# Attention and two MLPs on one core: a new order for the first batch, with its values and the second batch's keys summed by TensorE

## The chip, the cores and the metric

One core of one Trainium2 chip runs the whole program in one launch. The metric is the device time in microseconds; the kernel before was timed three times, with a median of 1646.4 us (1645.67 to 1647.27).

## The reference

```python
k_p = k.reshape(B, H, Sp, 8, D).mean(axis=3)      # B 8, H 8, S 576, D 64, Sp 72
v_p = v.reshape(B, H, Sp, 8, D).mean(axis=3)
scores = scale * np.matmul(q, k_p.transpose(0, 1, 3, 2))
attn = softmax(scores)
x = np.matmul(attn, v_p)                          # to [4608, 512]
x = np.maximum(0.01 * h, h) @ w_out               # h = x @ w_in, 512 -> 2048 -> 512
out = (r * r) @ w_out2                            # r = max(x @ w_in2, 0)
```

All is in float32. Keys and values are averaged over groups of eight rows before the attention.

## The kernel before, in words

The program has three stages: attention (eight batches), the first MLP and the second MLP. Their work is interleaved: the first MLP walks over tiles of 512 tokens and 16 slices of the weights (`first`, L316 to L318 into `h`, and `second`, L316 to L318 into `acc`), and between its slices the loop draws steps from the generator `attention()` at a fixed rate. The first batch has nothing to hide behind, since the first MLP needs its result. Its order is written out by hand in `first_batch`, and `in_order` binds the instructions of every engine to that written order.

For one batch, 576 queries go in five chunks that start at 0, 128, 256, 320 and 448; the tile names carry this number. The keys of a batch come as two main tiles of 128 rows by 2 by 512 (`k`, L408) and a rest of four small loads (`rk`, L403), since 72 pooled rows for each of two heads are 16 more than 128. `pooled` adds eight rows to one with three VectorE additions (L368, L374). `pooled_pe` does the same on TensorE: for each main tile it adds eight products with the identity matrix in PSUM (`kp` and `vp`, L381), which the trace records as 16 matmuls. `prepare_k` then transposes the sums (`trk`, `trr`, L422, L437) and copies them into `kT`.

Stage a transposes a chunk of queries (`trq`, L540), and ScalarE copies it to `qT` (L544). The steps of `stage_parts`, called `b(i)` in the list, are: scores on TensorE (`s`, L561); the maximum on VectorE (`mx`, L571); eight exponentials on ScalarE (L578); sum, reciprocal (L590, L591) and the products `p` on GpSimd (L593, L601). `c1` and `c2` transpose `p` back (`pt`, `pr`) and split it into a high part by ScalarE and a low part by VectorE (L614, L615, L626, L628). `d` multiplies with the values (`o`), and L652 and L657 split the result into `xh` and `xl`, which `first` reads. `w(f)` is one step of decoding weight slice f: L204, L208, L211, L215 and L225 on VectorE and L224 on ScalarE. `split_weights` makes the two parts of a slice (`hl_in`, L243, L244).

Loads are issued by SyncE's queue, except the first main keys, which ScalarE's queue issues. `first_batch` uses VectorE for the first keys and values; the second batch's keys and values are summed on TensorE (`K_ON_PE`, `V_ON_PE`), at that time between the matmuls of the first MLP.

Of the kernel before, what the change touches and what calls it, by code (L numbers as in the profile page):

```python
# [17 lines left out]
P = 128  # L18
# [14 lines left out]
def attention_two_mlps(  # L33
# [21 lines left out]
    NF = DFF // P  # L55
    SPANS = (320, 256)
    EARLY = 5
    V_ON_PE = (1,)
    K_ON_PE = (1,)
    AHEAD = 5  # L60
    RATES = (2.5, 5.25)
# [259 lines left out]
    def attention():  # L321

        with ExitStack() as s:
# [70 lines left out]
            def load_kv(b, src, nm, issue=None):  # L394

                groups = src[b].rearrange("(m a) (kk j) d -> (a kk) m (j d)", a=2, j=POOL)
                rest = kv_tile(b, NP * RX, 1, f"r{nm}{b}")
                main = [kv_tile(b, P, 2, f"{nm}{b}_{g}") for g in range(2)]
                KV[nm, b] = rest, main

                def load_rest():
                    for m in range(NP):
                        nc.sync.dma_start(out=rest[m * RX:(m + 1) * RX, 0], in_=groups[P:, m])  # L403

                if nm == "v" or b == 0:
                    load_rest()
                for g in range(2):
                    (issue or nc.sync).dma_start(out=main[g], in_=groups[0:P, 2 * g:2 * g + 2])  # L408
                if nm == "k" and b > 0:
                    load_rest()  # L410

            KV = {}

# [7 lines left out]
            def turned(tr, kd, m):  # L421
                nc.tensor.transpose(tr[:, m * P:(m + 1) * P], kd[:, m].rearrange("p i d -> p (i d)"), ident)  # L422
# [20 lines left out]
            def prepare_k(b):  # L443
                kr, kk = KV.pop(("k", b))
                i = b % 2
                kd = ap1.tile([P, NP, 2, D], F32, tag="kd", name=f"kd{b}")
                if b == 0:
                    pooled(rr[:, 1:2], kr)
                if b in K_ON_PE:
                    for ps in pooled_pe(f"kp{b}", kk):  # L450
                        yield
                    nc.scalar.copy(kd, ps.unsqueeze(2).to_broadcast([P, NP, 2, D]))
                else:
                    for g in range(2):
                        pooled(kd[:, 2 * g:2 * g + 2], kk[g])
                        if b > 0:
                            yield
                            continue
                        tr = work("trk0") if g == 0 else tr
                        for m in range(2 * g, 2 * g + 2):  # L460
                            turned(tr, kd, m)
                        yield
                if b > 0:
                    pooled(rr[:, 1:2], kr)
                    load_v(b)
                    tr = work(f"trk{b}")
                    for m in range(NP):
                        turned(tr, kd, m)
                put_keys(i, tr, slice(0, NP))
                put_rest(i, b)  # L470
                yield
# [57 lines left out]

            qn, qt = {}, {}  # L530

            def load_q(b, span, at, off, n):
                qn[b, at] = qp.tile([P, H, D], F32, tag="q", name=f"q{b}_{at}", bufs=3)
                nc.sync.dma_start(out=qn[b, at][:n], in_=q[b, :, at:at + n, :].rearrange("h p d -> p h d"))

            def stage_a(b, span, at, off, n):
                t = qn.pop((b, at))
# [130 lines left out]

            nch = len(chunks) // B

            def first_batch():
# [4 lines left out]
                def q_in(i):  # L676
                    load_q(*chunks[i])
# [12 lines left out]
                def c2(i):  # L690
                    rest_part(*chunks[i])

                def d(i):
                    if i not in rows:
                        rows[i] = stage_d(*chunks[i][:2])
                    next(rows[i])
                    put_stores(made)

                def w(f):
                    if f not in dec:  # L700
                        dec[f] = decode_steps(f)
                    next(dec[f], None)

                def fetch(f):
                    RAW[f] = fetch_weights(1, [("in", f), ("out", f)])

                load_k(0)
                q_in(0)
                q_in(1)
                load_v(0)  # L710
                q_in(2)
                next(pk)
                a(0)
                next(pk)
                next(pk)
                a(1)
                q_in(3)
                q_in(4)
                fetch(0)
                next(pv)  # L720
                fetch(1)
                b(0)
                b(0)
                b(1)
                b(1)
                b(0)
                next(pv)
                b(1)
                b(0)
                a(2)  # L730
                next(pv)
                b(1)
                a(3)
                b(2)
                b(2)
                next(pv)
                b(2)
                b(2)
                c1(0)
                b(3)  # L740
                b(3)
                c2(0)
                c1(1)
                c2(1)
                next(pv)
                a(4)
                q_in(5)
                q_in(6)
                q_in(7)
                load_k(1)  # L750
                c1(2)
                c2(2)
                b(3)
                b(4)
                b(4)
                w(0)
                b(3)
                d(0)
                d(0)
                b(4)  # L760
                w(0)
                b(4)
                d(0)
                d(0)
                w(0)
                w(0)
                fetch(2)
                c1(3)
                c2(3)
                c1(4)  # L770
                c2(4)
                split_weights("in", 0, 0)
                w(1)
                w(1)
# [12 lines left out]
                w(2)  # L787
                w(2)
                a(5)
                a(6)  # L790
# [1 line left out]
            marks.append(in_order(first_batch))  # L792
            ready[0] = 1
            yield
            yield from prepare_k(1)
            stage_b(*chunks[nch])
            yield
            def finish(i):
# [516 lines left out]
```

## Time and profile before

| | |
|---|---|
| median of 3 runs | 1646.4 us |
| the profiled execution | 1644.78 us |
| its span | 1643.1 us |
| TensorE busy in the span | 1604.8 us (98%) |
| VectorE busy | 1391.3 us (85%) |
| ScalarE busy | 1006.9 us (61%) |
| first matmul of the first MLP | at 43.85 us |

The span is what the instructions fill; 1.7 us of the execution lie around it. Busy time of TensorE holds time in which a matmul waits in its pipeline, so what matters is where it stands idle. In the first 44 us it is often idle, and from then on hardly ever.

### The profile page before, as it was taken

The page shows a single profiled execution, that of the slowest core. Times are in us where ns is not written, and L with a number is a line of the kernel's source. Part 1 is how long each engine was busy: PE and PEld are TensorE (multiplying, and loading weights), DVE is VectorE, ACT ScalarE, POOL GpSimd, SP SyncE. Part 2 cuts the span into 40 slices and gives each one's busy share as a digit, 9 for nine tenths or more (in the row PEclk, how much of TensorE's full clock was granted, in tenths as well). Part 3 has the DMA queues.
Part 4 walks back from the last instruction along what each step waited for, and adds up shares of the span by engine and source line. Part 5 has one row for each costly group of instructions (what it writes and reads, how often), then busy time and mean ns, then how long its engine had stood idle before and what let it go on. Part 6 is the DMA issues. An engine that isn't in the chain of part 4 may idle for free.

```text
span 1643.1 us, 25946 instructions
## 1 busy us (share of the span) xinstructions
PE 1604.8 (98%) x9048; PEld 1469.3 (89%) x9048; DVE 1391.3 (85%) x2062; ACT 1006.9 (61%) x1922; POOL 122.8 (7%) x152
## 2 busy tenths in 40 slices
PE   5999999999999999999999999999999999999999
PEld 4877788888888999999999998998998998998997
DVE  6999776889889989979759589789789799799687
ACT  6787677755667867667556546446456456455454
POOL 4121232213210000000000000000000000000000
PEclk9999999999999999999999999999999999999999
DMA  7665445776647689887766755865865766756655
GB/s 210 201 200 156 145 137 155 219 221 208 187 147 266 244 273 303 256 308 226 226 195 202 235 185 143 287 193 148 274 189 173 259 180 193 243 173 207 198 167 167
DMA packets 223090, 340.94 MB, mean 207 GB/s; under 512 B 55536, under 2 KB 137456, under 8 KB 222960
## 3 DMA queue, kind: packets, MB, share of 16 engines
q1 hardware_dynamic: 222416, 338.23, 66.3%
q8 instruction: 72, 1.18, 0.3%
q10 hardware_dynamic: 544, 1.05, 0.2%
q14 instruction: 58, 0.48, 0.1%
HBM read 268.44 MB, written 69.21 MB: 205 GB/s over the span
## 4 chain that ended last, share of the span: by engine, by line
PE 79%; DVE 11%; ACT 4%; DMA 3%; issue 2%; SPq 0%; POOL 0%; DVEq 0%; ACTq 0%; POOLq 0%
PE psum L1087 14%; PE psum L316 13%; PE psum L318 13%; PE psum L317 13%; PE psum L1088 7%; PE h L316 3%; PE h L318 2%; PE h L317 2%; PE acc L317 2%; PE acc L318 2%; PE acc L316 2%; ACT x L578 2%; DMA wb_in<-ws_in 1%; PE s L561 1%; DVE gl L874 1%
## 5 line engine op out<-in xcount | busy, mean ns | idle before, releaser
L1087 PE MATMUL psum<-wb_out,oh 128*128 128x512 f32 x1008 | 352.9, 394 | 0.0
L316 PE MATMUL psum<-xh,wb_in 128*128 128x384 f32 x1008 | 337.4, 335 | 3.1 <-ACT s L1061 1.5
L318 PE MATMUL psum<-xh,wb_in 128*128 128x384 f32 x1008 | 336.8, 334 | 0.0
L317 PE MATMUL psum<-xl,wb_in 128*128 128x384 f32 x1008 | 336.8, 334 | 0.0
L939 ACT CAST oh<-g 128x768 fp32r<-128x768 f32 x252 | 210.1, 836 | 157.5 <-PE psum L1087 91.1
L1088 PE MATMUL psum<-wb_out,ol 128*128 128x256 f32 x1008 | 281.8, 280 | 0.0
L940 DVE TENSOR_TENSOR ol<-g,oh 128x768 fp32r<-128x768 f32 x252 | 238.7, 951 | 16.3 <-ACT oh L939 14.1
L1087 PEld LDWEIGHTS psum<-wb_out,oh 128*128 128x128 f32 x1008 | 189.6, 188 | 43.3
L316 PEld LDWEIGHTS psum<-xh,wb_in 128*128 128x128 f32 x1008 | 189.2, 188 | 5.0 <-DVE g L1067 2.0
L317 PEld LDWEIGHTS psum<-xl,wb_in 128*128 128x128 f32 x1008 | 189.2, 188 | 0.2
L318 PEld LDWEIGHTS psum<-xh,wb_in 128*128 128x128 f32 x1008 | 189.2, 188 | 0.0
L1088 PEld LDWEIGHTS psum<-wb_out,ol 128*128 128x128 f32 x1008 | 188.8, 187 | 0.2
L993 ACT CAST wb_in<-wb_in 128x512 fp32r<-128x512 f32 x144 | 89.3, 621 | 146.3 <-DMA wb_in<-ws_in 142.2
L994 DVE TENSOR_TENSOR wb_in<-wb_in 128x512 fp32r<-128x512 f32 x144 | 98.5, 687 | 81.4 <-ACT wb_in L993 81.2
L943 DVE TENSOR_TENSOR g<-g,g 128x768 f32<-128x768 f32 x144 | 135.7, 950 | 1.5 <-ACT g L1015 0.9
L316 PE MATMUL h<-xh,hl_in 128*128 128x512 f32 (+1 forms) x320 | 121.5, 380 | 2.7 <-ACT hl_in L243 1.0
L317 PE MATMUL acc<-gl,hl_out 128*128 128x512 f32 (+1 forms) x320 | 119.0, 374 | 3.0 <-DVE gl L874 3.0
L316 PE MATMUL acc<-gh,hl_out 128*128 128x512 f32 (+1 forms) x320 | 121.0, 384 | 0.8 <-ACT gh L873 0.7
L318 PE MATMUL acc<-gh,hl_out 128*128 128x512 f32 (+1 forms) x320 | 118.7, 374 | 0.0
L318 PE MATMUL h<-xh,hl_in 128*128 128x512 f32 (+1 forms) x320 | 118.7, 371 | 0.0
L317 PE MATMUL h<-xl,hl_in 128*128 128x512 f32 (+1 forms) x320 | 118.0, 369 | 0.0
L317 PE MATMUL psum<-ol,wb_out 128*128 128x384 f32 x336 | 112.6, 335 | 0.0
(162 smaller groups left out, 3122.8 us busy)
## 6 DMA issues: line engine op xcount, KB each, us to landing
wb_in<-wd_in SPq DMA_DIRECT2D x108, 512.0 KB, 3.7
wb_out<-wd_out SPq DMA_DIRECT2D x108, 512.0 KB, 4.4
wb_in<-ws_in SPq DMA_DIRECT2D x144, 256.0 KB, 3.1
wb_out<-ws_out SPq DMA_DIRECT2D x144, 256.0 KB, 2.7
xs<-x SPq DMA_DIRECT2D x18, 768.0 KB, 5.6
out_dram<-o SPq DMA_DIRECT2D x23, 384.0 KB, 5.3
q<-in_q_dram SPq DMA_DIRECT2D x32, 256.0 KB, 3.8
v<-in_v_dram SPq DMA_DIRECT2D x16, 512.0 KB, 4.2
```

The source lines that it names most:

```text
L316: nc.tensor.matmul(outp, ah, bh, start=first, stop=False, **kw)
L317: nc.tensor.matmul(outp, ah, bl, start=False, stop=False, **kw)
L318: nc.tensor.matmul(outp, al, bh, start=False, stop=last, **kw)
L561: nc.tensor.matmul(sc[:n, 2 * m:2 * m + 2].rearrange("p a x -> p (a x)"), qT[:, 2 * e + m, :n], kT[b % 2][:, 2 * e + m].rearrange("p a x - ...
L578: nc.scalar.activation(x[:n, 4 * e + h], sc[:n, h], AF.Exp, bias=mx[:n, h], accum_out=sm[:n, 4 * e + h],)
L939: nc.scalar.copy(hi, src)
L940: nc.vector.tensor_tensor(out=lo, in0=src, in1=raw(hi), op=ALU.subtract)
L943: nc.vector.tensor_tensor(out=out_, in0=a, in1=b, op=ALU.subtract)
L993: nc.scalar.copy(whole[:, 0], raw(whole[:, 1]))
L994: nc.vector.tensor_tensor(out=whole[:, 1], in0=raw(whole[:, 1]), in1=raw(whole[:, 0]), op=ALU.subtract)
L1087: nc.tensor.matmul(outp, ah, b, start=first, stop=False, skip_group_check=True)
L1088: nc.tensor.matmul(outp[:, 1], al, b[:, 0], start=False, stop=last, skip_group_check=True)
```

## The change

The loads of the main keys and values go ahead of their rests, and the first chunk of queries is issued by ScalarE's queue. VectorE sums the main keys first and the rest after them. TensorE begins with 18 transposes of the identity matrix into a tile that nobody reads (`run_in`). The values of the first batch are summed on TensorE (`vp`), and so are the keys of the second batch (`kp`) before the first MLP begins. The written order of the first batch is new.

```diff
-    V_ON_PE = (1,)
+    V_ON_PE = (0, 1)
...
-                if nm == "v" or b == 0:
-                    load_rest()
                 for g in range(2):
                     (issue or nc.sync).dma_start(out=main[g], in_=groups[0:P, 2 * g:2 * g + 2])
-                if nm == "k" and b > 0:
-                    load_rest()
+                for m in range(NP):
+                    nc.sync.dma_start(out=rest[m * RX:(m + 1) * RX, 0], in_=groups[P:, m])
...
-                if b == 0:
-                    pooled(rr[:, 1:2], kr)
...
-                        tr = work("trk0") if g == 0 else tr
-                        for m in range(2 * g, 2 * g + 2):
-                            turned(tr, kd, m)
-                        yield
-                if b > 0:
-                    pooled(rr[:, 1:2], kr)
+                pooled(rr[:, 1:2], kr)
+                if b == 0:
+                    yield
+                else:
                     load_v(b)
...
+                def run_in(n):
+                    idle = work("run_in")[:, 0:P]
+                    for _ in range(n):
+                        nc.tensor.transpose(idle, ident, ident)
...
                 load_k(0)
-                q_in(0)
+                q_in(0, nc.scalar)
                 q_in(1)
                 load_v(0)
+                run_in(18)
...
+                load_k(1)
+                pk1.append(prepare_k(1))
...
-            yield from prepare_k(1)
+            yield from pk1[0]
```

The line numbers fall by 11 in the part that the prediction speaks of (L561 becomes L550). Three places show the new order. First TensorE, between the scores of the second chunk and the transposes of the third. Before:

```order
L561 MATMUL s_128_0_294<-kT_184,qT_128_252 128x144 x2
L561 MATMUL s_128_1_297<-kT_184,qT_128_252 128x144 x2
L540 MATMUL trq_256_329<-ident,q_256_218 128x64 x4
L540 MATMUL trq_320_345<-ident,q_320_254 128x128 x4
L561 MATMUL s_256_0_355<-kT_184,qT_256_334 64x144 x2
```

And now:

```order
L550 MATMUL s_128_0_296<-kT_184,qT_128_271 128x144 x2
L550 MATMUL s_128_1_299<-kT_184,qT_128_271 128x144 x2
L381 MATMUL vp_330<-v_0_210,ident 128x128 x8
L381 MATMUL vp_330<-v_1_211,ident 128x128 x8
L529 MATMUL trq_256_347<-ident,q_256_237 128x64 x4
L550 MATMUL s_256_0_371<-kT_184,qT_256_352 64x144 x2
```

The sums of the values stand ahead of the third chunk's transposes. Next ScalarE, from the exponentials of the first chunk to those of the third. Before:

```order
L578 ACTIVATE x_0_278,sm_0_279<-s_0_1_284,mx_0_1_289 128x72 x4
L578 ACTIVATE x_128_291,sm_128_292<-s_128_0_294,mx_128_0_300 128x72 x4
L578 ACTIVATE x_128_291,sm_128_292<-s_128_1_297,mx_128_1_302 128x72 x4
L544 COPY qT_256_334<-trq_256_329 128x4x64
L544 COPY qT_320_350<-trq_320_345 128x512
L507 ACTIVATE vM_186<-vd_261,side_of 128x4x64 x2
```

And now:

```order
L567 ACTIVATE x_0_280,sm_0_281<-s_0_1_286,mx_0_1_291 128x72 x4
L533 COPY qT_256_352<-trq_256_347 128x4x64
L567 ACTIVATE x_128_293,sm_128_294<-s_128_0_296,mx_128_0_318 128x72 x4
L567 ACTIVATE x_128_293,sm_128_294<-s_128_1_299,mx_128_1_320 128x72 x4
L496 ACTIVATE vM_186<-vp_330,side_of 128x4x64 x2
L533 COPY qT_320_390<-trq_320_385 128x512
```

The copy of the third chunk's transposes (`qT_256`) now stands ahead of the second chunk's exponentials. Last VectorE, at the end of the first batch, where `pt_l` of the fifth chunk (448) is what the last products `o` wait for. Before:

```order
L225 ISA w_0_477<-wm_0_478,w_0_477 128x2048
L615 TENSOR_TENSOR pt_l<-pt_320_536,pt_h 128x4x128
L628 TENSOR_TENSOR pt_r<-pr_320_543,pt_r 32x2x128
L615 TENSOR_TENSOR pt_l<-pt_448_548,pt_h 128x4x128
L628 TENSOR_TENSOR pt_r<-pr_448_555,pt_r 32x2x128
L244 TENSOR_TENSOR hl_in_0_560<-w_0_477,hl_in_0_560 128x512
L204 TENSOR_SCALAR wm_1_564<-st_in_out_275 128x1024
```

And now:

```order
L225 ISA w_0_406<-wm_0_407,w_0_406 128x2048
L579 TENSOR_SCALAR sm_448_481<-sm_448_481 128x8
L580 RECIPROCAL rs_448_482<-sm_448_481 128x8
L604 TENSOR_TENSOR pt_l<-pt_320_575,pt_h 128x4x128
L617 TENSOR_TENSOR pt_r<-pr_320_582,pt_r 32x2x128
L244 TENSOR_TENSOR hl_in_0_587<-w_0_406,hl_in_0_587 128x512
L204 TENSOR_SCALAR wm_1_599<-st_in_out_315 128x1024
L208 TENSOR_SCALAR wm_1_599<-wm_1_599 128x1024
L211 TENSOR_SCALAR wm_1_599<-wm_1_599 128x1024
L604 TENSOR_TENSOR pt_l<-pt_448_603,pt_h 128x4x128
```

The sums of chunk 448 now stand behind L225, and the split of the weights and three steps of the next slice's decoding stand between them and `pt_l`.

## Rows read from the trace of the kernel before

**Rows 1.** The page: busy time, share of the span and instructions of the engines.

```profile
PE 1604.8 (98%) x9048; PEld 1469.3 (89%) x9048; DVE 1391.3 (85%) x2062; ACT 1006.9 (61%) x1922; POOL 122.8 (7%) x152
```

**Rows 2.** Windows: start and end, length, busy us (instructions) by engine, clock, DMA share, GB/s.

```profile
15.00:35.00 20.00, 14.05 (x86) 11.61 (x85) 16.65 (x40) 18.68 (x97) 10.23 (x14) 0.91 0.80 219
35.00:44.00 9.00, 5.82 (x23) 4.47 (x24) 8.63 (x14) 4.35 (x13) 3.60 (x3) 0.62 0.38 124
50.00:160.00 110.00, 106.17 (x538) 87.31 (x537) 107.09 (x166) 88.89 (x207) 20.40 (x18) 0.98 0.61 192
```

**Rows 3.** Waits up to 70 us: who for whom, us in all, times, longest.

```profile
PE trk L422 <- DVE kd L374: 9.9, 1, 9.9
```

**Rows 4.** Loads of main keys, then of the first two query chunks: issue times, landing.

```profile
L408 ACTq DMA_DIRECT2D k<-in_k_dram x2: 443/465/487, 0.8 to 1.3; - x2
...
DMA to landing us min/median/max: 3.8/4.7/5.5
L534 SPq DMA_DIRECT2D q<-in_q_dram x2: 424/600/777, 2.6 to 3.1; - x2
...
DMA to landing us min/median/max: 5.4/5.9/6.4
```

**Rows 5.** Timeline, 8 to 18 us: start, length, engine, line, work [idle before].

```profile
8.14 1.14 DVE L368 TENSOR_TENSOR k<-k 128x512 f32<-128x512 f32 x2
9.31 0.42 DVE L374 TENSOR_TENSOR kd<-k 128x256 f32<-128x256 f32 x1
12.23 1.11 PE L540 MATMUL trq<-ident,q 128*128 128x128 f32 x4
13.14 3.75 PE L561 MATMUL s<-kT,qT 128*128 128x144 f32 x16
14.96 0.32 ACT L578 ACTIVATE x<-s,mx 128x72 f32<-128x72 f32 x1 [0.99 <-DVE mx L571]
16.82 1.05 PE L540 MATMUL trq<-ident,q 64*128 64x64 f32 x8
```

**Rows 6.** Windows of 2 us, 18 to 22 us, as in rows 2.

```profile
18.00:20.00 2.00, 0.00 (x0) 0.00 (x0) 1.86 (x7) 2.00 (x15) 0.72 (x1) 0.93 0.90 325
20.00:22.00 2.00, 1.78 (x8) 1.65 (x8) 1.93 (x5) 1.28 (x4) 1.59 (x4) 0.50 0.71 213
```

**Rows 7.** Timeline of TensorE, later scores of 128 rows.

```profile
23.20 1.15 PE L561 MATMUL s<-kT,qT 128*128 128x144 f32 x8
```

**Rows 8.** Timeline of ScalarE, 17 to 35 us.

```profile
17.34 0.36 ACT L578 ACTIVATE x<-s,mx 128x72 f32<-128x72 f32 x1
21.37 0.91 ACT L507 ACTIVATE vM<-vd,side_of 128x256 fp32r<-128x256 f32 x2 [0.72 <-DVE vd L374]
27.71 0.37 ACT L614 CAST pt_h<-pt 128x256 fp32r<-128x256 f32 x1 [0.39 <-PE pt L613]
34.45 1.21 ACT L224 ACTIVATE w<-st_in_out 128x1024 uint32<-128x1024 uint32 x1
```

**Rows 9.** Timeline of VectorE and TensorE, 37 to 44 us.

```profile
37.18 1.22 DVE L225 CUSTOM_DVE_ANT_0 w<-wm,w 128x2048 uint16<-128x2048 uint16 x1
39.48 0.69 DVE L615 TENSOR_TENSOR pt_l<-pt,pt_h 128x512 fp32r<-128x512 f32 x1
41.26 0.69 DVE L204 TENSOR_SCALAR wm<-st_in_out 128x1024 uint32<-128x1024 uint32 x1
40.23 0.58 PE L317 MATMUL o<-pt_l,vM 128*128 128x256 f32 x1 [0.53 <-DVE pt_l L615]
43.85 0.50 PE L316 MATMUL h<-xh,hl_in 128*128 128x512 f32 x1
```

**Rows 10.** Timeline inside the first MLP: pooling on TensorE, and what follows it.

```profile
72.43 3.73 PE L381 MATMUL vp<-v,ident 128*128 128x128 f32 x32
75.92 0.47 PE L316 MATMUL h<-xh,hl_in 128*128 128x512 f32 x1
```

**Rows 11.** Waits of TensorE, 40 to 160 us.

```profile
PE acc L317 <- DVE gl L874: 2.4, 1, 2.4
```

More of the change, by code (lines that the diff above doesn't have):

```diff
@@ L399, in load_kv @@
                 KV[nm, b] = rest, main
-                def load_rest():
-                    for m in range(NP):
-                        nc.sync.dma_start(out=rest[m * RX:(m + 1) * RX, 0], in_=groups[P:, m])
-                if nm == "v" or b == 0:
-                    load_rest()
                 for g in range(2):
                     (issue or nc.sync).dma_start(out=main[g], in_=groups[0:P, 2 * g:2 * g + 2])
-                if nm == "k" and b > 0:
-                    load_rest()
+                for m in range(NP):
+                    nc.sync.dma_start(out=rest[m * RX:(m + 1) * RX, 0], in_=groups[P:, m])
             KV = {}
@@ L457, in prepare_k @@
                             yield
-                            continue
-                        tr = work("trk0") if g == 0 else tr
-                        for m in range(2 * g, 2 * g + 2):
-                            turned(tr, kd, m)
-                        yield
-                if b > 0:
-                    pooled(rr[:, 1:2], kr)
+                pooled(rr[:, 1:2], kr)
+                if b == 0:
+                    yield
+                else:
                     load_v(b)
-                    tr = work(f"trk{b}")
-                    for m in range(NP):
-                        turned(tr, kd, m)
+                tr = work(f"trk{b}")
+                for m in range(NP):
+                    turned(tr, kd, m)
                 put_keys(i, tr, slice(0, NP))
@@ L530, in attention, with load_q @@
             qn, qt = {}, {}
-            def load_q(b, span, at, off, n):
+            def load_q(b, span, at, off, n, issue=None):
                 qn[b, at] = qp.tile([P, H, D], F32, tag="q", name=f"q{b}_{at}", bufs=3)
-                nc.sync.dma_start(out=qn[b, at][:n], in_=q[b, :, at:at + n, :].rearrange("h p d -> p h d"))
+                (issue or nc.sync).dma_start(out=qn[b, at][:n], in_=q[b, :, at:at + n, :].rearrange("h p d -> p h d"))
             def stage_a(b, span, at, off, n):
@@ L669, in attention @@
             nch = len(chunks) // B
+            pk1 = []
             def first_batch():
@@ L674, in first_batch, with q_in @@
                 dec, rows = {}, {}
-                def q_in(i):
-                    load_q(*chunks[i])
+                def q_in(i, issue=None):
+                    load_q(*chunks[i], issue)
                 def a(i):
@@ L713, in first_batch @@
                 a(0)
-                next(pk)
                 next(pk)
@@ L724, in first_batch @@
                 b(1)
+                next(pv)
+                fetch(1)
                 b(1)
@@ L727, in first_batch @@
                 next(pv)
-                b(1)
-                b(0)
[L730 to L733, printed above, removed]
+                next(pv)
+                a(2)
+                b(1)
+                b(0)
                 b(2)
@@ L736, in first_batch @@
                 next(pv)
+                a(3)
                 b(2)
-                b(2)
-                c1(0)
+                b(1)
+                w(0)
                 b(3)
                 b(3)
+                c1(0)
                 c2(0)
+                load_k(1)
+                pk1.append(prepare_k(1))
+                b(3)
+                b(2)
                 c1(1)
@@ L746, in first_batch @@
                 a(4)
+                w(0)
+                b(4)
+                b(4)
+                c1(2)
+                c2(2)
+                b(4)
+                b(3)
+                w(0)
+                d(0)
+                d(0)
+                d(0)
+                d(0)
+                w(0)
+                fetch(2)
                 q_in(5)
@@ L749, in first_batch @@
                 q_in(7)
[L750 to L753, printed above, removed]
-                b(4)
[L755 to L767, printed above, removed]
+                next(pk1[0])
+                b(4)
                 c1(3)
                 c2(3)
+                split_weights("in", 0, 0)
+                next(pk1[0])
+                w(1)
+                w(1)
                 c1(4)
                 c2(4)
-                split_weights("in", 0, 0)
-                w(1)
-                w(1)
                 d(4)
```

2 lines of the change are left out of this document (removed).

## The prediction, as it was made before the run

> **What bounds the kernel now.** I read the page first: TensorE is busy for 98% of the span and the next engine for 85% [rows 1]. After the first 50 us a microsecond is therefore worth gaining only where TensorE loses it. Two windows then tell where the change works [rows 2]. From 15 to 35 us ScalarE is busy for 18.68 of 20 us, TensorE for 14.05: ahead of the first MLP the exponentials bind. From 50 to 160 us TensorE has 106.17 of 110 us and VectorE 107.09: both are full, and relief for one alone is worth at most the 2.9 us that VectorE stands idle. The change works in the first stretch and takes work from TensorE in the second. Its worth is the time at which the first matmul of the first MLP starts, 43.85 us now [rows 9], and what the stream gains after that.
>
> **Step 1, the keys.** TensorE's first wait is for the summed keys, 9.9 us [rows 3]. The main keys land at 0.8 + 3.8 = 4.6 and 1.3 + 5.5 = 6.8 us [rows 4]. Summing one tile takes 1.14 + 0.42 = 1.6 us [rows 5]. With the rest no longer first, the second sum is ready at about 8.4 us, where it was ready after 11 before. But the new order puts the first chunk's transposes ahead of the keys', and these need its queries. Now the two query loads land at 2.6 + 5.4 = 8.0 and 3.1 + 6.4 = 9.5 us [rows 4]. The first one becomes third in ScalarE's queue behind a megabyte of keys, so I bound it by these two and take 9.0. From there TensorE has 4 + 4 + 1 + 4 transposes, 0.9 us for four (12.23 to 13.14, rows at the low clock) [rows 5]: 2.9 us, and the scores start at 12.0 instead of 13.14. The exponentials of the first chunk begin 1.8 us after the scores (13.14 to 14.96) [rows 5], so at 13.8 instead of 14.96: a gain of 1.2 us, ending at 16.2, since eight take 17.34 - 14.96 = 2.4 us [rows 5, 8].
>
> **Step 2, the values on TensorE.** Here the change gives back. It removes six VectorE additions, which were beside other work except for a wait of 0.72 us before `vM` [rows 8]. It adds 32 matmuls. The same `vp` of a later batch takes 3.5 us at the full clock (72.43 until the next `h` at 75.92) [rows 10]. They stand ahead of the third chunk's transposes; ScalarE's copy of those stands ahead of the second chunk's exponentials. So ScalarE, the binding engine, waits for scores, `vp` and transposes. What that takes depends on the clock. Sixteen score matmuls took 3.75 us at 13.14, 0.234 each, and eight took 1.15 at 23.20, 0.13 to 0.14 each [rows 5, 7]: the first ran at the lower level (1.2 of 2.4 GHz), though the granted clock shows a fall only at 20 us. TensorE had worked since 9.9 us, and 16.82 is where rows are fast (eight transposes in 1.05); the second time the clock was 0.50 from 20 to 22 us, and the scores at 23.20 are fast [rows 5, 6, 7]. The new stream begins at 9.1 and has no pause. I take the rise between 3 us later (12.1, as from 20.2 to 23.2) and 6.9 us later (16.0, as from 9.9 to 16.8), in the middle 14.0. The scores then end at 15.0 (8.5 of them slow, 7.5 fast), `vp` at 18.5, the transposes half a microsecond later (half of the eight at 16.82), the copy at 19.4. The bounds by the same count are 18.5 and 20.2. The second chunk's exponentials thus start at 19.3 instead of 17.34: **+2.0 us**. The 1.2 us of step 1 are inside this number.
>
> **Step 3, from there to the decoding of slice 0.** The same ScalarE work follows, with four differences. One copy is already done: -0.4 (a cast of its size takes 0.37 [rows 8]). The wait for the VectorE sums is gone: -0.7. `vM`'s second half now waits for a VectorE step in between, since both read PSUM: +0.5, an estimate from the 0.45 us that each half takes [rows 8]. And `pt_h` of the third chunk now waits behind eight scores (1.15) and four transposes (0.5) where it had waited 0.4 [rows 5, 7, 8]: +1.2. Sum **+0.6 us**; ScalarE's L224 starts at 34.45 + 2.6 = 37.05.
>
> **Step 4, from there to the first MLP.** Now VectorE's `pt_l` of the last chunk starts at 39.48, 5.0 us after L224 [rows 8, 9]. In the new order VectorE has after L224 (1.2 us): L225 with `pt_l` and `pt_r` of 320, as before (37.18 to 39.48, 2.3), the split (0.7, as `pt_l` of its size) and L204, L208, L211 (0.7 each as the first of them), and two short sums of chunk 448, for which I allow 0.4 [rows 8, 9]: 6.7 us, **+1.7 us**. Before, these three lay beside the last products. Those run from 40.23 to 43.85, 3.6 us, at a granted clock of 0.62 from 35 to 44 us [rows 2, 9]. With the second keys' `kp` ahead of them TensorE idles less; the full clock can give back at most half of 3.6. Between 0 and -1.8 I take -1.2, since 0.62 / 1 of 3.6 leaves 2.2 and the first of them still wait. **+0.5 us**. The first matmul of the MLP then starts at 43.85 + 2.0 + 0.6 + 0.5 = 46.95.
>
> **Step 5, inside the MLP.** The second keys' 32 matmuls leave the full stretch: 3.5 us by the `vp` rows [rows 10]. It counts wholly if TensorE is the bound and not at all if VectorE is; TensorE already waited 2.4 us for VectorE's `gl` there [rows 11]. VectorE can move up by at most its idle 2.9 us [rows 2]. I take the middle between 0 and 3.5: **-1.7 us**. Their cover before the MLP is TensorE's idle time while VectorE decodes; if that were gone they would cost there what they save here.
>
> **Other edits.** The 18 transposes of `run_in` take 18 x 0.22 = 4 us from about 1.6, and nothing waits for TensorE before 9 us [rows 3]: no cost. The value loads start once the keys have landed, and `vp` comes only at 15. The second keys are asked for some microseconds earlier and needed after 36 us: hidden.
>
> **Sum.** 2.0 + 0.6 + 0.5 - 1.7 = +1.4 us on the profiled execution of 1644.8 us. This execution lies 1.6 us below the median, so on the median it is 1646.4 + 1.4 = **1647.8 us**. A measurement of this kernel tells some 0.2%, 3.3 us, from no change.
>
> **The clock, weighed.** TensorE was idle from 18 to 20 us, and the granted clock of the next stretch was 0.50 [rows 6]. `run_in` ends near 5.6 us and the queries land at 8 or later, so I give it nothing for the scores. The Trainium skill (TensorE: Matmul & The Clock Gate, What's actually happening) says that throttled is the default and activity releases it; by that `run_in` would have released the clock, and the first scores would be fast, which is the first rival. The trace agrees as to the scores at 13.14, and it shows too that idling takes the clock back.
>
> **Rivals.**
> *The clock is up from the start.* `run_in` releases it, the queries land at 8.0, and TensorE keeps it. Then 13 transposes take 1.4 us, but `kT` needs the keys (8.4) and its copies, so scores start at 10.2 and end at 12.3, `vp` at 15.8, the second exponentials start at 16.8: -0.5. With steps 3 and 4 unchanged the MLP starts at 44.45, and TensorE is the bound after it: -3.5. Sum -2.9, or 1643.5; with 0.6 us less in step 4 (its bound of -1.8), 1642.9. For it: TensorE is full from 50 us. Against: the idle gap after `run_in`.
> *VectorE decides* (the other side). The queries land at 9.5, the clock rises late: second exponentials at 20.5, +3.2; step 3 +0.6; the last products stay slow, +1.7; and in the MLP VectorE is the bound, so `kp` gives nothing. Sum +5.5, or 1651.9. It decides once VectorE's work in the 110 us from the MLP's start passes what TensorE's does; it is at 97% now. The second batch's attention also runs two steps earlier, which brings VectorE work into this stretch.
> *The rest of the MLP comes in another order.* Loads and attention steps shift against the slices until about 580 us, and TensorE's small waits there fall otherwise. That widens every case by a microsecond or two to either side.
>
> **How the numbers follow.** The forecast has a chance of 0.53, with its own range 1645 to 1650.5 from the bounds of steps 1 to 5. The first rival has 0.2, the second 0.27. Faster by over 0.2% means below 1643.1, slower above 1649.7. The first rival lies around the lower limit, and with the reordering most of its chance and a little of the forecast's lies below: 0.18. The second gives most of its chance to slower, and the forecast its upper end: 0.28. The rest, 0.54, is within. The range from 1642.4 to 1651.6 leaves out the ends of both rivals.
>
> **What would show it.** In the profile after: `trq` of the first chunk near 9 us; the keys' sum ready by 8.5; `vp` between the scores and `trq` of the third chunk, 3.5 to 4 us long; ScalarE waiting 2 to 4 us for PE `trq` ahead of the third chunk's copy, and 1.6 us ahead of the third `pt_h`; the second exponentials near 19.3; first `h` near 47. Step 5 shows in TensorE's waits for `gl` between 45 and 160 us: more than 2.4 us means that VectorE took back part of `kp`. I am wrong if the first scores run at 0.13 us each, if `h` starts before 44 us, or if the MLP's first 16 slices last over 2 us longer than now.

## The result, and the profile after

The change makes the kernel slower: 1656.7 us against 1646.0 us for the kernel before on the same chip, ratio 1.007 with a 95% interval of 1.0055 to 1.0086 (the two medians alone give 1.0065). A later chip, with the same two kernels, gave 1.0074 (1.0059 to 1.0089). The forecast was 1647.8 us with a range to 1651.6; the time lies outside it, on the side of the second rival. Chips differ by some 3 us, so kernels are compared by their ratio to the kernel before on their own chip. One thousandth is 1.6 us.

The page's line of engines answers to [rows 1]. TensorE is busy 10.7 us more, with 50 instructions more (18 transposes of `run_in` and 32 matmuls of `vp`) and a mean granted clock of 0.992 instead of 0.996; VectorE 3.9 us less:

```profile
PE 1615.5 (98%) x9098; PEld 1480.8 (89%) x9098; DVE 1387.4 (84%) x2056; ACT 1005.5 (61%) x1922; POOL 125.0 (8%) x152
```

The windows that answer to [rows 2] show where work is missing. ScalarE, 18.7 us busy from 15 to 35 us before, is now busy 13.9, and TensorE in the first MLP 99.5 of 110 us instead of 106.2. The last two rows are stretches at the low level of the clock:

```profile
15.00:35.00 20.00, 12.44 (x79) 10.54 (x78) 12.17 (x29) 13.89 (x73) 8.07 (x12) 0.84 0.55 179
35.00:44.00 9.00, 8.73 (x56) 8.32 (x55) 6.63 (x12) 5.30 (x16) 4.74 (x6) 0.78 0.32 106
50.00:160.00 110.00, 99.48 (x480) 79.81 (x480) 104.06 (x158) 84.06 (x197) 25.71 (x18) 0.96 0.63 196
32.00:39.00 7.00, 6.11 (x26) 5.55 (x26) 5.24 (x13) 4.76 (x23) 2.54 (x3) 0.51 0.00 0
46.00:52.00 6.00, 5.25 (x20) 4.86 (x21) 3.34 (x7) 2.79 (x9) 0.00 (x0) 0.50 0.37 60
```

The timeline of the head answers to [rows 5, 7, 8, 9]. The first score, the second exponentials (18.02), L224, `pt_l` of chunk 448 (46.01) and the first `h` (50.14) are the marks of the prediction's steps:

```profile
11.29 2.41 PE L550 MATMUL s<-kT,qT 128*128 128x144 f32 x16
12.75 0.32 ACT L567 ACTIVATE x<-s,mx 128x72 f32<-128x72 f32 x1 [0.64 <-DVE mx L560]
13.53 3.73 PE L381 MATMUL vp<-v,ident 128*128 128x128 f32 x32
18.02 0.33 ACT L567 ACTIVATE x<-s,mx 128x72 f32<-128x72 f32 x1
...
30.69 1.25 PE L550 MATMUL s<-kT,qT 128*128 128x144 f32 x8 [3.03 <-ACT qT L533]
32.36 0.37 ACT L603 CAST pt_h<-pt 128x256 fp32r<-128x256 f32 x1 [1.72 <-PE pt L602]
35.71 0.24 ACT L567 ACTIVATION_READ_ACCUMULATOR x<-s,mx 128x1 f32 x1
38.79 1.15 ACT L224 ACTIVATE w<-st_in_out 128x1024 uint32<-128x1024 uint32 x1
39.97 1.23 DVE L225 CUSTOM_DVE_ANT_0 w<-wm,w 128x2048 uint16<-128x2048 uint16 x1 [0.56 <-ACT w L224]
41.12 0.16 DVE L579 TENSOR_SCALAR sm<-sm 128x8 f32<-128x8 f32 x1
43.66 0.59 ACT L603 CAST pt_h<-pt 128x512 fp32r<-128x512 f32 x1 [1.20 <-PE pt L602]
46.01 0.69 DVE L604 TENSOR_TENSOR pt_l<-pt,pt_h 128x512 fp32r<-128x512 f32 x1
50.14 0.63 PE L316 MATMUL h<-xh,hl_in 128*128 128x512 f32 x1
```

TensorE's waits from 40 to 180 us answer to [rows 11]. Where its longest wait was for `gl`, it now waits for split weights (`hl_in`, `hl_out`), that is for decoding and splitting on VectorE and ScalarE:

```profile
PE acc L316 <- ACT hl_out L243: 4.2, 2, 3.4
PE h L318 <- DVE hl_in L244: 3.5, 4, 1.8
PE o L317 <- DVE pt_l L604: 2.1, 1, 2.1
PE acc L317 <- DVE gl L873: 0.9, 1, 0.9
```

As a ruler inside the first MLP I use the split of `h` (`gl`) of a unit, that is of one weight slice for one tile of tokens, 80 in all; units 0 and 15 bound a stretch in which both kernels do the same 15 units. Its start and end are the ends of the following windows, first before, then after:

```profile
48.18:160.11 111.93, 107.55 (x544) 88.53 (x545) 109.02 (x168) 90.81 (x209) 20.40 (x18) 0.98 0.62 195
```

```profile
55.57:175.86 120.29, 110.22 (x536) 88.72 (x536) 115.03 (x179) 92.81 (x218) 27.23 (x19) 0.97 0.63 194
```

The same 15 units take 8.4 us longer, and VectorE (third figure) has 6.0 us more to do in them, in 179 instructions instead of 168. It is busy 96 to 97% of either stretch. So of the 12.9 us between the two spans (1643.1 and 1656.0), 7.4 are there at the first split, another 8.4 by the sixteenth, and 2.9 come back later.

This ruler has a fault: between two units the kernels do the same MLP work, but not the same attention steps. Attention work that only comes earlier counts as lost at unit 15. The last unit, 79, is free of that, since the last copy of an attention result (`xo`) starts at 481.1 us before and at 494.4 us in the change. These are all 80 splits (the first and the last start stand behind the three durations), before, in the change, and in the run e15 below:

```profile
L874 DVE TENSOR_TENSOR gl<-g,gh x80: 411/682/1640, 48.2 to 582.1; 128x512 fp32r<-128x512 f32 x64, 128x256 fp32r<-128x256 f32 x16
L873 DVE TENSOR_TENSOR gl<-g,gh x80: 411/684/1660, 55.6 to 596.1; 128x512 fp32r<-128x512 f32 x64, 128x256 fp32r<-128x256 f32 x16
L877 DVE TENSOR_TENSOR gl<-g,gh x80: 417/684/1781, 48.1 to 589.9; 128x512 fp32r<-128x512 f32 x64, 128x256 fp32r<-128x256 f32 x16
```

At unit 79 the change is 14.0 us late: 7.4 from the head and 6.6 from the MLP. Two questions follow: what delayed the head, and what made the MLP longer.

### The profile page after: what moved, and what is told of

It reads as the page before. It is cut to its first block, busy times and chain, and to the rows that moved or that the text cites. A ratio compares the mean times of both kernels' runs of the same rounds, so it can differ in the third digit from the quotient of the medians.

```text
span 1656.0 us, 26030 instructions
## 1 busy us (share of the span) xinstructions
PE 1615.5 (98%) x9098; PEld 1480.8 (89%) x9098; DVE 1387.4 (84%) x2056; ACT 1005.5 (61%) x1922; POOL 125.0 (8%) x152
## 4 chain that ended last, share of the span: by engine, by line
PE 75%; DVE 14%; ACT 5%; DMA 3%; issue 3%; SPq 0%; POOL 0%; ACTq 0%; DVEq 0%; POOLq 0%
PE psum L1086 14%; PE psum L316 13%; PE psum L318 13%; PE psum L317 13%; PE psum L1087 7%; PE h L316 2%; PE h L318 2%; PE h L317 2%; PE acc L316 2%; DVE gl L873 2%; PE acc L317 2%; ACT x L567 1%; PE s L550 1%; PE acc L318 1%; DVE hl_in L244 1%
## 5 line engine op out<-in xcount | busy, mean ns | idle before, releaser
L992 ACT CAST wb_out<-wb_out 128x512 fp32r<-128x512 f32 x144 | 89.2, 620 | 44.5 <-DMA wb_out<-ws_out 43.2
```

The source lines that it names most:

```text
L992: nc.scalar.copy(whole[:, 0], raw(whole[:, 1]))
```

## The experiments

Theory A: VectorE decides in the first units (up to unit 15), and the second batch's attention, two steps early because its keys' steps were taken out of the MLP, loads it. Theory D: in the head, ScalarE and VectorE run their queues in order, and the new order leaves them waiting. Against them stand `vp`, `kp` and the clock as causes of their own. All results in one table (ratio to the kernel before on the same chip with its 95% interval; first `h`, and splits of units 0, 15 and 79, in us of the profiled execution):

| kernel | ratio | interval | first `h` | unit 0 | unit 15 | unit 79 |
|---|---|---|---|---|---|---|
| before | 1 | | 43.85 | 48.18 | 160.11 | 582.09 |
| change | 1.0070 | 1.0055-1.0086 | 50.14 | 55.57 | 175.86 | 596.06 |
| e8_after | 1.0074 | 1.0059-1.0089 | 50.27 | 54.53 | 174.25 | 593.26 |
| e1_hold | 1.0055 | 1.0039-1.0070 | 48.59 | 53.73 | 168.60 | 589.49 |
| e15_two_early | 1.0036 | 1.0023-1.0050 | 43.00 | 48.09 | 166.40 | 589.89 |
| e5_tail | 1.0061 | 1.0046-1.0076 | 49.12 | 53.35 | 172.50 | 591.68 |
| e6_mid | 1.0066 | 1.0046-1.0087 | 47.12 | 52.40 | 171.91 | 590.55 |
| e7_all | 1.0022 | 1.0013-1.0031 | 46.10 | 50.34 | 164.79 | 586.65 |
| e3_values_dve | 1.0070 | 1.0047-1.0093 | 47.25 | 51.48 | 172.06 | 591.27 |
| e10_values_dve2 | 0.9999 | 0.9990-1.0008 | 43.89 | 48.12 | 161.92 | 583.51 |
| e2_keys_back | 1.0044 | 1.0028-1.0060 | 50.69 | 55.05 | 169.42 | 590.82 |
| e11_keys_back2 | 1.0017 | 1.0008-1.0026 | 45.88 | 51.05 | 164.28 | 585.15 |
| e12_no_run_in | 1.0031 | 1.0019-1.0042 | 46.71 | 50.94 | 167.57 | 588.86 |
| e4_keys_first | 0.9989 | 0.9980-0.9999 | 44.03 | 49.25 | 161.38 | 581.98 |
| e9_keys_first_pv | 0.9983 | 0.9974-0.9992 | 42.34 | 47.07 | 159.36 | 580.35 |
| e13_keys_run_in | 0.9985 | 0.9976-0.9994 | 43.75 | 49.25 | 161.86 | 582.35 |
| e14_hold_more | 1.0026 | 1.0015-1.0036 | 42.26 | 46.60 | 161.95 | 584.76 |

The marks of one execution scatter. e1 and e15 leave the head as it was, and their first `h` still comes 1.7 us before e8's and 0.9 us before that of the kernel before; the change and e8, the same kernel, differ by 2.8 us at unit 79. A difference of some 2 us between two marks is therefore not read as an effect.

The time from unit 0 to unit 79 follows the place of the attention, whatever the head did. It is 532.7 to 535.8 us with attention where the kernel before has it (before, e2, e4, e9, e11, e13), 535.4 to 537.9 with the second keys' steps gone and two empty steps in their place (e1, e7, e10, e12), 538.2 to 541.8 two steps early (the change, e8, e3, e5, e6, e15) and 538.2 two steps late (e14). These are single executions, and the change and e8 lie 1.8 us apart in this measure; the groups differ by more on average, though their edges nearly touch (e12 and e6, 537.9 and 538.2).

**The two early steps: e1_hold, e15_two_early.** e1 holds the attention back inside the changed kernel:

```diff
             yield from pk1[0]
+            yield
+            yield
```

> The changed kernel with the second batch's attention held back by two empty steps, so that inside the first MLP it stands against the units as in the kernel before; the head is untouched. Theory A (VectorE's work decides: attention two steps early brings about 5 us of VectorE work into the first 16 units): the split of h of unit 15 comes 4 to 5 us earlier than 175.9, time 1656.7 - 4.5 = 1652 us. Theory B (only the late head costs, the stretch after it lags because the weights' loads start late): unit 15 and the time stay within 1.5 us of the changed kernel, 1655 to 1658. First h at 50.1 us in both.

e15 does the reverse in the kernel before; the second keys' two steps are issued there together with the first attention step:

```diff
-            yield from prepare_k(1)
+            early = prepare_k(1)
+            next(early)
+            next(early)
+            yield from early
```

> The kernel before with the second batch's attention two steps early inside the first MLP (the two kp steps issued together with the first attention step), the head untouched. Theory A (VectorE's work between the splits of h of units 0 and 15 decides; 109.0 us before, 115.0 in the change): first h at 43.9 us, VectorE's busy time between these two splits 4 to 6 us more than 109.0, unit 15 at 163.5 to 166 instead of 160.1, time 1.0015 to 1.003 of the kernel before. Rival (the steps cost only behind a late head): unit 15 within 1.5 us of 160.1, time within 0.0008 of the kernel before.

The stretch from unit 0 to unit 15, first in e1, then in e15:

```profile
53.73:168.60 114.87, 107.27 (x521) 86.07 (x522) 109.73 (x170) 92.38 (x212) 20.07 (x19) 0.99 0.61 192
```

```profile
48.09:166.40 118.31, 112.25 (x562) 92.09 (x563) 113.61 (x178) 92.76 (x214) 20.95 (x19) 0.97 0.63 198
```

Holding takes VectorE's work back to 109.7 us and the stretch from 120.3 to 114.9. In the kernel before, two steps early raise it from 109.0 to 113.6, the stretch from 111.9 to 118.3, and the time by 3.6 thousandths, 5.9 us, with a head that is no later than before. These are the numbers that theory A forecast, with unit 15 and the price a little above its upper ends (166 us and 1.003), and the price does not need the changed head. The runs show the early steps as the cause, but not VectorE as the way. In e15 TensorE is busy 112.3 us in the stretch too, where it was 107.6 before, with 18 matmuls more. And of the 6.3 us by which e15's unit 15 is late, 2.0 are left at unit 43 (394.41 us against 392.43), while 7.8 stand at unit 79: most of the loss arises far behind the first sixteen units. In e1 unit 15 comes 5.7 us earlier than in e8, of which 0.8 are there at unit 0, and unit 79 3.8 us earlier; the ratio is 1.9 thousandths lower, some 3 us; the intervals of the two overlap. What comes into the stretch can be read from VectorE's groups, first of before, then of the change: two more maxima and two more pooling instructions of the values, 2.0 of the 6.0 us (a later batch's keys bring some 3 more); ahead of the values VectorE also waits 1.5 us for their load.

```profile
L571 DVE TENSOR_REDUCE mx<-s 128x4 f32<-128x288 f32 (+1 forms) x10 | 4.4, 451 | 0.4 <-PE s L561 0.3
L368 DVE TENSOR_TENSOR v<-v 128x512 f32<-128x512 f32 (+1 forms) x4 | 2.1, 534 | 0.0
```

```profile
L560 DVE TENSOR_REDUCE mx<-s 128x4 f32<-128x288 f32 (+1 forms) x12 | 5.2, 451 | 1.4 <-PE s L550 1.3
L368 DVE TENSOR_TENSOR v<-v 128x512 f32<-128x512 f32 (+1 forms) x6 | 3.3, 548 | 1.5 <-DMA v<-in_v_dram 1.5
```

**Later than before is no better: e14_hold_more.** e9 (below) with two empty steps behind `yield from prepare_k(1)`.

> e9 with the second batch's attention two steps later than in the kernel before. Theory A alone: VectorE's work between the splits of units 0 and 15 falls by 3 to 5 us from 109, unit 15 comes 2 to 4 us earlier than 159.4, time 1 to 3 us under e9. If TensorE or the decoded weights decide by then, or the steps come back behind unit 15: unit 15 up to 1 us earlier, time within 1 us of e9 or longer.

VectorE's work falls from e9's 108.95 to 106.2 us, about as theory A says, yet unit 15 comes 2.6 us later than in e9 and the time rises from 0.9983 to 1.0026:

```profile
46.60:161.95 115.35, 108.02 (x546) 88.00 (x547) 106.19 (x163) 90.64 (x208) 17.40 (x17) 1.00 0.59 185
```

In this stretch TensorE waits in several places, 2.3 us for `hl_in`, 1.7 us at a `pr`, 1.4 us for `pt_r`. At units 17 and 18 e14 is level with e9 again (175.17 against 176.30, 183.10 against 183.05), but with less attention done; the early units do not tell where the 4.4 us arise by which it is late at unit 79. Theory A is thus not borne out: less work for VectorE in the first units did not shorten the MLP. What exactly makes either place dear stays open; the order of attention steps against the units had been at a good point, and moving it by two steps cost 3.6 thousandths one way (e15) and 4.3 the other.

**The order in the head: e5_tail, e6_mid, e7_all, with e8_after beside them.** e5 puts the sums of chunk 448 among the first products, and its transposes ahead of the decoding of slice 1:

```diff
                 d(0)
                 d(0)
+                b(4)
                 d(0)
                 d(0)
...
                 next(pk1[0])
-                b(4)
                 c1(3)
                 c2(3)
+                c1(4)
+                c2(4)
                 split_weights("in", 0, 0)
...
                 w(1)
                 w(1)
-                c1(4)
-                c2(4)
```

> The changed kernel with the last stretch before the MLP in the order of the kernel before: the probabilities of chunk 448 among the first products, its transposes and splits ahead of the decoding of slice 1 on VectorE. Theory D (order of the head on VectorE: the sums of chunk 448 wait from 37.3 to 41.1 us behind the decoding of slice 0, and its second split behind that of slice 1): first h 2 to 3.5 us earlier than in the changed kernel, time 2 to 4 us less. Rival E (the clock: a shorter wait only lets TensorE stay at the low level longer, as with the second keys taken out): first h less than 1 us earlier, time within 1.5 us.

e6 moves the exponentials of chunk 320 behind the transposes of chunk 448 and the casts of chunks 128 and 256:

```diff
-                b(3)
                 b(2)
                 c1(1)
                 c2(1)
                 next(pv)
                 a(4)
+                c1(2)
+                c2(2)
+                b(3)
                 w(0)
                 b(4)
                 b(4)
-                c1(2)
-                c2(2)
```

> The changed kernel with ScalarE's middle order of the kernel before: transposes of chunk 448 and the probabilities of chunks 128 and 256 cast before the exponentials of chunk 320. Theory D: TensorE no longer waits 3 us for the copy of chunk 448, the first product starts 1.5 to 2.5 us before 32.8 us, first h 1 to 2 us earlier, time 1 to 2.5 us less. Rival E: the low clock stands there all the same, first h less than 0.7 us earlier, time within 1 us.

e7 is both, and e1's two empty steps.

> Both orders together, and the second batch's attention held two steps back as in e1: what is left of the change is keys first, values and second keys on TensorE, and the early run of transposes. Theory A and D together: first h at 45 to 47 us, split of h of unit 15 at 162 to 166 us, time 1.000 to 1.003 of the kernel before. If the loss sits in vp, kp or the clock instead: first h over 48 us and 1.004 or more.

> The changed kernel itself once more, as the mark for the three beside it on the same chip: first h near 50 us, split of h of unit 15 near 175 us, ratio 1.007 to the kernel before.

Against e8 on the same chip, e5's first `h` is 1.2 us earlier (less than theory D's 2 to 3.5, and within the scatter of the marks), e6's 3.2 us (more than its 1 to 2); the times fall by 1.3 and 0.8 thousandths, about 2 and 1 us, which their intervals can't tell from nothing. In e5 this decides neither for theory D nor for the clock. The sum is clear: e7 is 5.2 thousandths under e8, 8.5 us, with first `h` at 46.1 and unit 15 at 164.8, inside what A and D expected. By the marks 4.2 us of this are there at unit 0, 6.6 at unit 79. In e7 the sums of chunk 448 stand ahead of L225 and its `pt_l` ahead of L204; `pt_l` starts at 41.15 instead of 46.01:

```profile
37.04 0.16 DVE L579 TENSOR_SCALAR sm<-sm 128x8 f32<-128x8 f32 x1
...
38.27 1.64 DVE L225 CUSTOM_DVE_ANT_0 w<-wm,w 128x2048 uint16<-128x2048 uint16 x1
...
41.15 0.69 DVE L604 TENSOR_TENSOR pt_l<-pt,pt_h 128x512 fp32r<-128x512 f32 x1
```

**The values: e3_values_dve, e10_values_dve2.** One line, `V_ON_PE = (1,)`, in the change and in e7.

> The changed kernel with the first values pooled by VectorE again, the order otherwise as in the change. Theory A (the 32 vp matmuls lie beside ScalarE's exponentials; the head is lost later, by the order of the copies on ScalarE and of the decoding on VectorE): first h within 1.5 us of 50.1, time within 1.5 us of 1656.7 or up to 2 us longer for three microseconds more of VectorE. Rival (vp on TensorE is the cost, my step 2): first h 2 to 3.5 us earlier, time 1653 to 1655.

> e7 with the first values pooled by VectorE again. If vp on TensorE ahead of the third chunk's transposes is most of what e7 still loses (step 2; e3 had its first h 2.9 us earlier than the change): first h 2 to 3 us before 46.1, time 1.5 to 3 us under e7, 0.9995 to 1.001 of the kernel before. Rival (vp is hidden, VectorE pays for the sums again): first h within 1 us of 46.1 and time within 1 us of e7.

In both, first `h` comes earlier, by 2.9 us against the change and 2.2 us against e7. In e3 the ratio does not show it (1.0070, as the change), but it can't deny it either: three of its four executions took 1653 us and one 1658.7, its interval is the widest of all, and at unit 79 it is 2.0 us ahead of e8, within the scatter. With the order of e7 it shows: e10 is at 0.9999, 2.3 thousandths or 3.8 us under e7. So `vp` ahead of the third chunk costs about what step 2 feared (2.0 us, and 2.2 at the first `h`). With values on VectorE, order restored and attention held, the change costs nothing that these runs can tell.

**The second keys: e2_keys_back, e11_keys_back2.** The two `next(pk1[0])` are left out of the first batch, in the change and in e7 (there without the empty steps).

> The changed kernel with the second keys' 32 matmuls back in the first MLP (loaded early as in the change). It also holds attention at the place of the kernel before. Theory A (VectorE decides in the MLP; kp before the MLP stands in TensorE's queue ahead of the transposes of chunk 320 and 448): first h 1 to 2.5 us earlier than 50.1, unit 15 at 168 to 171 instead of 175.9, time 1649 to 1652. Theory C (TensorE decides in the MLP, my step 5): kp costs there what it cost ahead of it, so first h earlier by up to 2.5 us but the time not under 1655.

> e7 with the second keys' 32 matmuls back in the first MLP (attention then stands as in the kernel before without the empty steps). Theory A (VectorE decides in the MLP, so kp is worth nothing there): time within 1.5 us of e7, or up to 2 us less if kp delays the transposes of chunk 320 ahead of the MLP. Step 5 of the prediction (kp early is worth 1.7 us, up to 3.5): time 1.5 to 3.5 us over e7.

e2's first `h` was expected 1 to 2.5 us earlier and is 0.5 us later, although 32 matmuls are gone ahead of it; its time is 3.0 thousandths under e8's, where e1's is 1.9 under it, and the intervals of e1 and e2 overlap. e11 and e7 overlap (1.0017 and 1.0022). Step 5's gain of 1.7 us for `kp` out of the MLP does not show, and a cost ahead of it doesn't either.

**Keys first and the early transposes: e4, e9, e13, e12.** e4 is the kernel before with the loads of the change (main keys, then the rest; first queries on ScalarE's queue) and its `prepare_k` for the first batch.

> The kernel before with one part of the change alone: main keys asked for and summed first, rest later, first queries asked for on ScalarE's queue; order, values and second keys as before. Step 1 of the prediction: first exponentials 1.2 to 2.2 us before 14.96 us. If the gain reaches the MLP: first h at 42 to 42.7 (43.85), time 1644.2 to 1645.2. If it is lost in a wait behind it (values, chunk 256's scores, the weights): first h within 0.6 of 43.85, time within 1 us of 1646.

The scores start at 10.95 us instead of 13.14, but the first exponentials at 14.88, as before: VectorE stood waiting for the rest of the values, and the maxima queued behind it. The first `h` is no earlier (44.03), and yet the time is 0.9989 of the kernel before, some 1.8 us less; where these come from, the marks do not show.

```profile
13.49 0.73 DVE L368 TENSOR_TENSOR rv<-rv 64x256 f32<-64x256 f32 x2 [4.60 <-DMA rv<-in_v_dram]
14.26 0.22 DVE L374 TENSOR_TENSOR rd<-rv 64x64 f32<-64x64 f32 x1
14.40 0.81 DVE L560 TENSOR_REDUCE mx<-s 128x4 f32<-128x288 f32 x2
```

e9 takes away that wait, by the order of the change:

```diff
                 fetch(0)
-                next(pv)
-                fetch(1)
                 b(0)
                 b(0)
                 b(1)
+                next(pv)
+                fetch(1)
                 b(1)
                 b(0)
```

> As e4 (the kernel before with the keys first), and the pooling of the rest of the values moved on VectorE behind the maxima of the first chunk, where the changed kernel has it: in e4 VectorE stood 4.6 us before that pooling, and the first exponentials waited 3.1 us for maxima behind it. Theory D (order ahead of the MLP is worth its wait): first exponentials at 12 to 12.9 us (14.88 in e4), decoding of slice 0 on ScalarE 1 to 2 us before 34.65, first h at 42 to 43.3, time 0.997 to 0.9985 of the kernel before. Rival F (the gain ends in a later wait, the values or the clock): first h within 0.7 us of 44.03, time 0.9985 to 1.0.

The maxima now go first (12.73), the exponentials start at 13.22 (expected at 12 to 12.9), L224 at 32.95, `h` at 42.34. The time is 0.9983 of the kernel before, 2.6 us less, and the interval excludes 1: this version beats both kernels, though by less than what one measurement of this kernel tells from no change. Its interval overlaps that of e4.

```profile
12.73 0.95 DVE L560 TENSOR_REDUCE mx<-s 128x4 f32<-128x288 f32 x2 [3.54 <-PE s L550]
13.60 0.72 DVE L368 TENSOR_TENSOR rv<-rv 64x256 f32<-64x256 f32 x2
```

e13 adds the 18 transposes (`run_in`) to e9, e12 takes them out of e7.

> e9 with the 18 transposes at the start. If they bring the clock up earlier: sixteen scores of the first chunks at least 0.4 us shorter than in e9, first exponentials 0.3 to 0.8 us earlier, first h 0.3 to 1 us earlier, time 0.3 to 1.5 us under e9. If not: all within 0.3 us and the time within 0.8 us.

> e7 without the 18 transposes at the start. By the prediction (run_in gives nothing to the scores): sixteen scores take within 0.4 us of the 3.2 us in e7, second exponentials and first h within 0.7 us, time within 1 us. Rival (run_in releases the clock): scores at 3.7 us and a vp that starts slow, second exponentials 1 to 2.5 us later, time 1 to 2.5 us longer.

In e13 the exponentials start 0.8 us earlier but `h` 1.4 us later, at a clock of 0.64 from 20 to 44 us (0.73 in e9); the scores take 2.92 against 2.68 us. e12 has its exponentials and `h` 0.6 us later than e7. All times overlap: `run_in` is worth nothing that these runs can tell.

## Why the prediction was wrong

The marks divide the 12.9 us between the two spans; each figure is a difference of starts in the rows above and in [rows 8, 9], and of the table of marks.

| step | forecast | measured |
|---|---|---|
| 2, to the second exponentials (17.34 to 18.02) | +2.0 | +0.7 |
| 3, from there to L224 (17.1 to 20.8 long) | +0.6 | +3.7 |
| 4, from L224 to the first `h` (9.4 to 11.35 long) | +0.5 | +1.95 |
| 5, first `h` to the split of unit 79 (538.2 to 545.9) | -1.7 | +7.7 |
| unit 79 to the end | 0 | -1.1 |

**Step 1 was right in mechanism, and better than said**: scores at 11.3, exponentials at 12.75, against 12.0 and 13.8. **Step 2** too: `vp` lies between the scores and the third chunk's transposes, 3.73 us long, and ScalarE waits 2.5 us for them. Its size was too large by 1.3 us (19.3 against 18.02). Of these, 0.7 come from the scores' earlier start and most of the rest from their shorter time, 2.4 us where I had 3.0: the granted clock was 0.57 from 8 to 12 us and full from 12 to 16, so it rose some 2 us earlier than the middle that I took. e10 confirms that `vp` is a cost.

**Step 3 failed with "the same ScalarE work follows".** The work is the same, but ScalarE's waits from 18 to 39 us rose; first in the change, then before (17.3 to 34.5 us):

```profile
ACT pt_h L603 <- PE pt L602: 2.5, 2, 1.7
...
ACT xh L641 <- PE o L636: 1.3, 2, 0.6
ACT vM L496 <- DVE vM L497: 0.6, 1, 0.6
ACT x L567 <- DVE mx L560: 0.5, 1, 0.5
```

```profile
ACT vM L507 <- DVE vd L374: 0.7, 1, 0.7
ACT pt_h L614 <- PE pt L613: 0.4, 1, 0.4
ACT pt_r L626 <- PE pr L625: 0.2, 1, 0.2
```

That is 4.9 us against 1.3, nearly the whole 3.7 (the wait for the third chunk's transposes ended at 17.75 and belongs to step 2). I had priced the wait for the third `pt_h` (1.6 forecast, 1.7 measured) and the one at `vM` (0.5 and 0.6). Not priced were the first `pt_h` (0.75), the maxima of chunk 448 (0.5), and `xh` (1.3) behind products that no exponentials cover any more and that ran at the low level: TensorE had waited 3.0 us for chunk 448's `qT`, which now stood behind the exponentials of chunk 320, and from 32 to 39 us its clock was 0.51.

**Step 4** took VectorE's list for the path, and that was right: VectorE stood without a gap from L225 to `pt_l`. L224 to `pt_l` took 7.2 us, against 6.7 forecast and 5.0 before. The other way to `pt_l`, over the sums of chunk 448, GpSimd's product, the transposes and ScalarE's cast, ended at 44.25 with `pt_h`, 1.8 us before `pt_l` started; what held `pt_l` back was the decoding, L204 to L211, ahead of it. The sums waited as well: the Trainium skill (Perfetto Trace Analysis, Tensor Engine Instruction (MATMUL, LD_WEIGHTS)) states that VectorE and ScalarE are strict first-in, first-out, unlike TensorE's weight loads; the rows agree: the exponentials of that chunk were done at 35.95 us, and its sum ran at 41.12, right behind L225. The larger miss is the clock: I gave back 1.2 us for it, but from `pt_l` to the first `h` 4.1 us passed against 4.4 before, and the last products and the first six of `h` ran at 0.50 from 46 to 52 us. TensorE had waited 2.1 us for `pt_l` just before.

**Step 5 is the failure that decides.** It took the middle between two bounds for `kp`, a gain of 1.7 us, and left out what the steps' absence does: the units' rate draws attention by the number of steps, so without two of them everything behind comes earlier. The sentence stood in the second rival, without a price. e15 gives it alone: 5.9 us, about half of the 11 to 12 us. In the changed kernel the marks divide alike: the change and e8 are 7.4 and 6.4 us late at unit 0, and take 6.6 and 4.8 us longer than the kernel before from there to unit 79. e7 shows 8.5 us for order and rate together, and e10 another 3.8 for `vp`, which leaves nothing. The single runs e1, e5 and e6 do not divide the 8.5 more finely, since their intervals are as wide as their effects. By what engine or wait the early steps cost their time in the MLP stays open. The sign that I had named for it, more than 2.4 us of waits for `gl`, did not come (0.9 us); the waits stood at the split weights, 4.2 and 3.5 us.

The second rival had the right sign, in part by luck: its 3.2 us ahead of the second exponentials measured 0.7, and it counted the MLP as neutral, where most of the miss lay. Whether it was right in its engine, these runs do not show.

## What to carry to other kernels

When a step is taken out of a loop that doles out other work by counting steps, all the work behind it moves; put it back, or forecast what the move costs. Judge such a move at a mark behind which none of the moved work is left, since a mark in the middle counts as lost what only came earlier. In an order written by hand, price a moved instruction by what stands before and behind it on its own engine, not by its length: in e4 additions that waited for a load held back the maxima behind them, and the exponentials started 1.7 us later than in e9, where the maxima go first.

## What was not expected of the hardware

The same kernel, profiled twice (the change and e8), ran its first transposes and scores at different levels of the clock. First the change, then e8, each with two rows of TensorE's windows (span, busy, granted clock, DMA share, GB/s):

```profile
8.22 1.08 PE L529 MATMUL trq<-ident,q 128*128 128x128 f32 x4 [2.83 <-DMA q<-in_q_dram]
...
8.00:12.00 4.00, 3.77 (x17) 0.57 1.09 322
12.00:16.00 4.00, 4.00 (x37) 1.00 1.33 186
```

```profile
7.77 0.66 PE L529 MATMUL trq<-ident,q 128*128 128x128 f32 x4 [2.04 <-DMA q<-in_q_dram]
...
10.29 3.30 PE L550 MATMUL s<-kT,qT 128*128 128x144 f32 x16
...
8.00:12.00 4.00, 3.71 (x21) 0.66 1.11 318
12.00:16.00 4.00, 4.00 (x34) 0.92 1.29 227
```

In e8 the first transposes behind `run_in` ran at the full level; TensorE had waited 2 us ahead of them, the clock fell behind them (0.66 from 8 to 12 us), it was back later than in the change, and the sixteen scores took 3.30 us instead of 2.41. By the third chunk's transposes both stood at the same place (17.20 and 17.09 us). The Trainium skill (TensorE: Matmul & The Clock Gate, What's actually happening) says that the number of slow matmuls at a start differs from run to run of one kernel; these two executions agree.

Taking work off TensorE did not visibly bring it forward. Without `kp` in the head (e2) the clock was 0.57 from 44 to 52 us, against 0.62 over the same time in the change, and `h` started half a microsecond later, a difference within the scatter of this mark:

```profile
44.00:52.00 8.00, 6.36 (x28) 5.26 (x27) 5.24 (x11) 3.33 (x11) 1.24 (x2) 0.57 0.66 149
```
